# The first chunk's decay attention as blocks of 128 tokens, in a new order of steps

## The chip, the cores and the metric

The kernel runs on one core of a Trainium2 chip. The metric is device time in microseconds (us), the median over several executions. One more execution was taken by the hardware profiler, and every row below is from that one.

## What is computed

The input is q, k, v of 4 batches, 8 heads, 768 tokens and 64 values for each head, a decay `lam` for each head, and two weight matrices in float64. The attention is linear and causal, with a state that decays by `lam` for each token; its output x (3,072 tokens of 512 values) goes through a feed-forward layer of 2,048 hidden values with a softplus.

```python
for b in range(nb):                                   # blocks of 64 tokens
    intra = einsum('bhic,bhjc->bhij', qb, kb) * Dmask  # lam ** (i - j) where i >= j, else 0
    intra = einsum('bhij,bhjd->bhid', intra, vb)
    inter = einsum('bhid,bhde->bhie', qb * lam_pow, kv_state)
    out[:, :, sl] = intra + inter
    kv_state = lam_block * kv_state + einsum('bhsd,bhse->bhde', kb * rev_pow, vb)
x = out.transpose(0, 2, 1, 3).reshape(B * S, H * D)
h = x @ w_in
return softplus(h) @ w_out
```

Nothing in the sum over a block asks for 64 tokens: with a mask over 128 tokens the same result comes from a block of 128.

## The kernel before

The 768 tokens of each batch are cut into 6 chunks of 128, so that a chunk holds 512 tokens over the 4 batches. The attention of one chunk is done in 4 units, one for each pair of heads; unit g belongs to chunk g // 4. A unit's data is 1 MB in two loads of 512 KB (`att`): one with q and k, values along the partitions, one with k and v, tokens along the partitions. Within a unit each chunk is two halves of 64 tokens. `mm_scores` (step `xy`) makes the scores x of both halves and the states' updates y, `mask_scores` (`a`) multiplies the scores by the decay mask, `first_states` or `update_first` and `update_second` (`st`, `dl`, `uh`, `ul`) make the states, and `mm_out` (`z`) adds what comes from the state and from the scores. Before `mm_scores`, `k_decay` (`k`) multiplies k by its decay on ACT, or DVE for unit 0; before `mm_out`, `q_decay` (`q`) multiplies q on DVE. `x_high` (`xh`, ACT) and `x_low` (`xl`, DVE) write the output as two parts, each in the reduced float32 that TensorE reads at full rate (fp32r), so that a product takes three matmuls.

The weights come as float64, 512 KB for each of 16 slices of `w_in` (A0 to A15) and of `w_out` (B0 to B15). `scale` and `round` (ACT), `shift`, `sign` and `add` (DVE) turn the bits into float32, `hi` (ACT) and `lo` (DVE) split it into the two parts. `m f p` and `n f p` (`mlp1`, L412) are three 128x128x512 matmuls of slice f with pair p for chunks 0 and 1; `act`, `ghi`, `glo` are softplus and split of the result; `l2 f` (L425) is the second layer. `sum`, `ph`, `pl`, `snd`, `sA`, `sB` make sums of weight blocks for the later chunks and store them to DRAM, `L2` loads the second layer's weights from there.

All of chunks 0 and 1, and the attention of most later chunks, is issued in an order that is written out by hand as a table of 672 steps (670 after the change); it holds until 234 us. Each engine and each DMA queue takes its instructions in that order, and an instruction that waits holds up all behind it on its engine. Chunks 2 and 3 (pair 1) follow in a loop over 8 steps, in which seven products over block sums (P1 to P7, L593) stand in place of eight, with one unit of attention in each step (`event`). There `box_sums` (L518 and L503 to L506) and `box_parts` (L530) make sums of the second layer's weights on DVE. Chunks 4 and 5 run at last, with `out_product` (L958) for the second layer in the same seven products, in order P1, P6, P2, P7, P5, P4, P3.

SBUF tiles are taken from pools by size (`t8` has 21 buffers of 8 KB for each partition); PSUM has 4 banks `o`, 2 banks `h`, and one tile of 2 banks, `work`, for the outputs z of the units.

Of the kernel before, what the change touches and what calls it, by code (L numbers as in the profile page):

```python
# [15 lines left out]
C = 128  # L16
T = 64
# [13 lines left out]
def decay_attention_softplus_ffn(  # L31
# [103 lines left out]
    for word in "u0 A0 u1".split():  # L135
        load(word)

    spare = t8([128, 4, 512], F32, "spare")
# [15 lines left out]
    ramp = spare[:, 3, 0:T]  # L154
    for s in range(2):
        nc.gpsimd.iota(
            ramp[half(s)], pattern=[[1, T]], base=1 - T, channel_multiplier=1, allow_small_or_imprecise_dtypes=True
        )
    step, *begins = [spare[:, n].rearrange("q (h i) -> q h i", h=H) for n in range(3)]
    nc.gpsimd.memset(begins[1], 0.0)  # L160
    nc.gpsimd.memset(begins[1][:, :, 0:1], 1.0)
    nc.vector.tensor_single_scalar(
        out=begins[0], in_=ramp.rearrange("q (o i) -> q o i", o=1).broadcast_to([128, H, T]), scalar=0.0,
        op=ALU.is_equal,
    )
    nc.vector.tensor_copy(out=step, in_=lam_b.rearrange("q (h o) -> q h o", o=1).broadcast_to([128, H, T]))
    nc.vector.memset(step[:, :, 0:1], 0.0)

    mask = cp.tile([128, H, T], F32, name="mask")

    lp = cp.tile([128, H, T], F32, name="lp")

    def powers(out, n):
        nc.vector.tensor_tensor_scan(
            out=out.rearrange("q h i -> q (h i)"), data0=step.rearrange("q h i -> q (h i)"),
            data1=begins[n].rearrange("q h i -> q (h i)"), initial=0.0, op0=ALU.mult, op1=ALU.add,
        )


    rp1 = cp.tile([128, H], F32, name="rp1")  # L180
    lam_c = cp.tile([128, H], F32, name="lam_c")
    powers(mask, 0)
    nc.vector.tensor_mul(out=rp1, in0=mask[:, :, T - 1], in1=lam_b)
# [76 lines left out]
    def own(g, n, name):  # L260
        if not first_chunk(g):
            return t2([128, B, 2, 64], F32, f"{name}_{g}")
        if g not in spares:
            spares[g] = t8([128, 3, B, 2, 64], F32, f"own_{g}")
        return spares[g][:, n]

    def k_decay(g):
        kd = kds[g] = own(g, 0, "kd")
        if g == 0:
            w = rp1[:, heads(g)].rearrange("q (o t w) -> q o t w", o=1, w=1).broadcast_to([128, B, 2, D])  # L270
            nc.vector.tensor_mul(out=kd, in0=kt_of(g), in1=w)
            return
        for t in range(2):
            h = heads(g).start + t
            nc.scalar.activation(kd[:, :, t], kt_of(g)[:, :, t], AF.Copy, scale=rp1[:, h : h + 1])  # L275

    def q_decay(g):
        qd = qds[g] = own(g, 1, "qd")
        r = hi if first_chunk(g) else slice(0, 128)
        eng = nc.gpsimd if g < 2 else nc.vector  # L280
        w = lp[r, heads(g), :].rearrange("q (o t) i -> q o (t i)", o=1).broadcast_to([r.stop - r.start, B, 2 * T])
        eng.tensor_mul(
            out=qd[r].rearrange("q b t i -> q b (t i)"), in0=q_of(g)[r].rearrange("q b t i -> q b (t i)"), in1=w
        )


# [50 lines left out]
    def carry_states(g, y):  # L337
# [693 lines left out]
```

## Time and profile before

| | |
|---|---|
| median of 3 executions | 579.18 us (578.6 to 579.54) |
| the profiled execution's own time | 580.86 us |
| its span, first to last instruction | 578.8 us |
| TensorE matmuls (PE) | 562.5 us busy, 97% of the span |
| VectorE (DVE), ScalarE (ACT) | 382.8 and 274.2 us busy, 66% and 47% |
| mean granted TensorE clock | 0.993 |
| DMA | 149.70 MB, mean 259 GB/s |

The time of an execution holds 2.1 us beside the span. A busy PE says that a matmul is in flight, and matmuls overlap; what counts is when the next one can start. Idle time matters only on the engine that the others wait for.

### The profile page before, as it was taken

Reading aid. Unit: us, or ns where it says so; the run is one execution under the profiler, and the core shown is the slowest. Engines: PE = TensorE matmul, PEld = TensorE weight load, DVE = VectorE, ACT = ScalarE, POOL = GpSimd, SP = SyncE. Lnnn points to the kernel's source line nnn. Section 1 sums busy time; section 2 is a strip of 40 time slices with the busy share of each in tenths; the row PEclk is TensorE's granted clock in tenths of the full one; section 3 lists DMA queues with packets and bytes.
Section 4 is the critical chain, followed back from the end, with each engine's and each line's share of the span. In section 5 each row is a group of like instructions: output and inputs, shape, how many; then the busy total and the mean of one; then the engine's idle time right before and its main releaser. Section 6 shows DMA issues by size and latency. Waiting matters only on the chain.

```text
span 578.8 us, 12242 instructions
## 1 busy us (share of the span) xinstructions
PE 562.5 (97%) x5208; PEld 459.5 (79%) x5208; DVE 382.8 (66%) x593; ACT 274.2 (47%) x438; POOL 3.9 (1%) x10
## 2 busy tenths in 40 slices
PE   7699999999999999999999999999999999999997
PEld 6567888788887788887878888878888888788885
DVE  5998988687844688466556765549123646748983
ACT  3766668482826454254344443456032334454441
POOL 2000000000000000000000000000000000000000
PEclk9799999999999999999999999999999999999999
DMA  8997399579898899864785787797976246911711
GB/s 289 407 406 303 121 351 340 189 251 330 292 349 326 280 374 398 332 227 193 224 296 172 233 314 228 286 318 290 420 258 221 106 140 212 383 46 59 269 37 73
DMA packets 52678, 149.70 MB, mean 259 GB/s; under 512 B 4496, under 2 KB 20880, under 8 KB 46480
## 3 DMA queue, kind: packets, MB, share of 16 engines
q1 hardware_dynamic: 41040, 135.28, 64.6%
q10 hardware_dynamic: 11584, 13.63, 6.7%
q8 instruction: 41, 0.67, 0.5%
q14 instruction: 13, 0.11, 0.0%
HBM read 111.15 MB, written 37.75 MB: 257 GB/s over the span
## 4 chain that ended last, share of the span: by engine, by line
PE 87%; DMA 8%; DVE 2%; issue 1%; ACT 1%; SPq 1%; ACTq 0%
PE o L425 28%; PE h L412 15%; PE rP L958 13%; PE b L593 11%; PE c L593 7%; PE a L593 7%; DMA att<-in_att 3%; PE x L294 2%; DMA w<-g 2%; PE z L309 2%; DMA raw<-in_wts 2%; PE z L313 1%; PE y L296 1%; DMA out_dram<-ob 1%; DVE box L518 0%
## 5 line engine op out<-in xcount | busy, mean ns | idle before, releaser
L425 PE MATMUL o<-w,g 128*128 128x512 f32 x768 | 185.9, 393 | 0.6 <-DMA w<-g 0.6
L425 PEld LDWEIGHTS o<-w,g 128*128 128x128 f32 x768 | 142.4, 188 | 32.0 <-DMA w<-g 1.1
L412 PE MATMUL h<-x,w 128*128 128x512 f32 x384 | 93.6, 394 | 0.2 <-ACT x L357 0.2
L412 PEld LDWEIGHTS h<-x,w 128*128 128x128 f32 x384 | 70.8, 188 | 16.5 <-ACT x L357 0.6
L958 PE MATMUL rP<-sP,vP 128*128 128x512 f32 x336 | 76.3, 389 | 0.0
L958 PEld LDWEIGHTS rP<-sP,vP 128*128 128x128 f32 x336 | 63.1, 188 | 13.1
L593 PE MATMUL b<-xcP,w1b 128*128 128x512 f32 x192 | 49.1, 391 | 1.2 <-DVE act L895 0.8
L593 PE MATMUL a<-xcP,w1a 128*128 128x512 f32 x192 | 48.8, 389 | 0.0
L326 DVE SCALAR_TENSOR_TENSOR st<-st,lam_c,y 64x256 f32<-64x256 f32 x80 | 35.2, 479 | 14.3 <-PE y L296 13.2
L593 PEld LDWEIGHTS b<-xcP,w1b 128*128 128x128 f32 x192 | 35.8, 188 | 9.8 <-DVE ta L751 1.2
L593 PEld LDWEIGHTS a<-xcP,w1a 128*128 128x128 f32 x192 | 36.0, 188 | 7.6
L321 DVE TENSOR_TENSOR a<-x,mask 128x512 f32<-128x512 f32 x20 | 13.8, 690 | 35.0 <-PE y L296 18.2
L294 PE MATMUL x<-att 64*64 64x64 f32 x768 | 30.7, 226 | 0.0
L294 PEld LDWEIGHTS x<-att 64*64 64x64 f32 x768 | 27.2, 139 | 4.3 <-issue 3.2
L604 DVE TENSOR_TENSOR g<-lb,g 128x512 fp32r<-128x512 f32 x32 | 21.6, 687 | 11.3 <-ACT g L600 11.3
L600 ACT CAST g<-lb 128x512 fp32r<-128x512 f32 x32 | 19.3, 618 | 20.0 <-PE o L425 12.3
L275 ACT ACTIVATE kd<-att,rp 128x256 f32<-128x256 f32 x40 | 18.2, 502 | 20.5 <-DMA att<-in_att 10.3
L895 DVE TENSOR_TENSOR act<-b,ta 128x512 f32<-128x512 f32 x8 | 5.5, 692 | 31.1 <-PE b L593 31.1
L838 ACT CAST sP<-act 128x512 fp32r<-128x512 f32 x32 | 19.2, 619 | 13.0 <-PE rP L958 6.8
L604 DVE TENSOR_TENSOR sP<-act,sP 128x512 fp32r<-128x512 f32 x32 | 20.9, 687 | 6.5 <-ACT sP L838 6.5
L296 PE MATMUL y<-att,kd 64*64 64x64 f32 x576 | 23.1, 220 | 1.5 <-ACT lb L401 1.2
L593 PE MATMUL c<-xcP,w1b 128*128 128x512 f32 x96 | 24.4, 389 | 0.0
(124 smaller groups left out, 791.8 us busy)
## 6 DMA issues: line engine op xcount, KB each, us to landing
att<-in_att SPq DMA_DIRECT2D x48, 512.0 KB, 8.0
w<-g SPq DMA_DIRECT2D x24, 1024.0 KB, 8.3
raw<-in_wts SPq DMA_DIRECT2D x32, 512.0 KB, 10.1
w1a<-g SPq DMA_DIRECT2D x16, 1024.0 KB, 7.1
g<-w SPq DMA_DIRECT2D x24, 512.0 KB, 7.4
w1b<-g SPq DMA_DIRECT2D x16, 768.0 KB, 7.0
g<-box SPq DMA_DIRECT2D x16, 512.0 KB, 9.4
vP<-box ACTq DMA_DIRECT2D x32, 256.0 KB, 6.1
```

Source lines behind the costliest of these rows:

```text
L275: nc.scalar.activation(kd[:, :, t], kt_of(g)[:, :, t], AF.Copy, scale=rp1[:, h : h + 1])
L294: nc.tensor.matmul(x[r, cols], lhsT=k[r, b, t], rhs=q[r, b, t], start=True, stop=True)
L296: nc.tensor.matmul(y[half(1 - s), cols], lhsT=kd[r, b, t], rhs=v[r, b, t], start=True, stop=True,)
L321: nc.vector.tensor_mul(out=a, in0=x.rearrange("q (b t i) -> q b t i", b=B, t=2), in1=m)
L326: nc.vector.scalar_tensor_tensor(out=to[:, :, t], in0=of[:, :, t], scalar=lam_c[r, h : h + 1], in1=u[:, :, t], op0=ALU.mult, op1=ALU.add,)
L412: nc.tensor.matmul(to, lhsT=w[:, i, cs], rhs=x[:, j, :], start=not done and n == 0, stop=len(done) == NP - 1 and n == 2,)
L425: nc.tensor.matmul(outs[c, b], lhsT=g[:, i, b * 128 : (b + 1) * 128], rhs=w[:, j], start=k == 1 and n == 0, stop=k == NF and n == 2,)
L593: nc.tensor.matmul(to, lhsT=w[:, k, n, p * 128 : (p + 1) * 128], rhs=x[:, j, p], start=start and p == 0 and m == 0, stop=p == 1 and m == 2 ...
L600: nc.scalar.copy(out=g[:, 0], in_=l)
L604: nc.vector.tensor_sub(out=g[:, 1], in0=l, in1=g[:, 0])
L838: nc.scalar.copy(out=g[:, 0], in_=of)
L958: nc.tensor.matmul(to, lhsT=w[:, k, x, n * 128 : n * 128 + 128], rhs=g[:, y], start=fresh and i == 0 and m == 0, stop=i == NF // 2 - 1 and ...
```

## The change

Chunk 0's four units take their 128 tokens as one block. The input's layout for them is changed to match on the host, q and k with one head on each half of the partitions, k and v with all 128 tokens along the partitions. `first_scores` makes scores of 128x128 (64 partitions in, 128 columns of weights, 128 columns streamed) into two PSUM banks, one for each head, and y with 128 partitions in and 64 columns; `first_mask` multiplies by a mask of 128 positions, in two instructions; `first_out` has 128 partitions in and 64 columns of weights. No state is needed within the chunk: steps `q 0` to `q 3` and `dl 0` to `dl 3` are gone, and the state that goes to chunk 1 is a copy of y in two instructions. The masks are made over 1,024 columns first (`mask1`, `rpa`), and the ones for 64 tokens after them (`lpset`, `mk64`, `rp1`).

The softplus results of chunk 0's slices 0 to 3 have a buffer of their own (`early`), where one tile held each in turn. The table of steps is a new one. In pair 1 the sums over the second layer's weights of step i are made in step i + 1 in two parts, and `q_decay` follows `event`. Before the last two products P4 and P3 of chunks 4 and 5, one `out_product` of slice 0 is issued ahead of each.

```diff
-        for major in range(2):
+        for major in (1, 0) if g == 0 else (0, 1):
...
-    for word in "u0 A0 u1".split():
+    for word in "".split():
...
+    def first_scores(g, xs, y):
+        q, k = [units[g][:, 0, n].rearrange("q (b i) -> q b i", b=B) for n in range(2)]
+        kd, v = kds.pop(g), part(g, 1, 1)
+        for b in range(B):
+            for t in range(2):
+                r = half(t)
+                nc.tensor.matmul(xs[t][:, b * C : (b + 1) * C], lhsT=k[r, b], rhs=q[r, b], start=True, stop=True)
+        for b in range(B):
+            for t in range(2):
+                nc.tensor.matmul(y[half(t), b * D : (b + 1) * D], lhsT=kd[:, b, t], rhs=v[:, b, t], start=True, stop=True)
+
+    def first_mask(g, xs):
+        a = aa[g] = own(g)[:, 1:3].rearrange("q t (b i) -> q t b i", b=B)
+        for t in range(2):
+            h = heads(g).start + t
+            m = mask1[:, h : h + 1].broadcast_to([128, B, C])
+            nc.vector.tensor_mul(out=a[:, t], in0=xs[t].rearrange("q (b i) -> q b i", b=B), in1=m)
+
+    def first_out(g, w):
+        a, v = aa.pop(g), part(g, 1, 1)
+        for b in range(B):
+            for t in range(2):
+                nc.tensor.matmul(
+                    w[half(t), 0, b * C : (b + 1) * C], lhsT=v[:, b, t], rhs=a[:, t, b], start=True, stop=True
+                )
...
-        st = states[g] = states[g + NP] = th([128, B, 2, D], F32, f"st_{g}")
-        nc.scalar.copy(out=st[hi].rearrange("q b t d -> q (b t d)"), in_=y[hi])
+        st = states[g + NP] = th([128, B, 2, D], F32, f"st_{g}")
+        for t in range(2):
+            nc.scalar.copy(out=st[lo, :, t], in_=y[half(t), 0:256].rearrange("q (b e) -> q b e", b=B))
...
-        l_tiles[f] = tl([128, 512], F32, f"l{f}")
+        if not early:
+            early.append(t8([128, 4, 512], F32, "l0"))
+        l_tiles[f] = early[0][:, f] if f < 4 else tl([128, 512], F32, f"l{f}")
...
-        scale A0, q 0, L A1, L B4, L u3, q 1, k 0, xy 0, L u2, st 0, round A0, L A3, L A2, L A6, L A4, L A5, shift A0,
+        mk64, L A0, lpset, round A0, L u0, L A1, L u1, k 0, scale A0, shift A0, sign A0, scale A1, xy 0, add A0, L u2,
...
-                q_decay(unit)
...
             if i >= 1:
-                box_parts(box_at[i - 1])
+                box_full(box_at[i - 1])
...
             low_of(ga, la)
+            if i >= 1:
+                box_four(box_at[i - 1])
...
                 event(unit)
+                if unit < NG:
+                    q_decay(unit)
                 nxt += 1
             low_of(gb, c21)
...
-            box_sums(box_at[i])
+            if i >= 1:
+                box_parts(box_at[i - 1])
...
-    run(late)
+    banks = {}
+    for n in range(2):
+        banks["a", n] = obank(f"rP1_{n}")
+        out_product("P1", 0, n)
+        run(late, 1)
```

Three places of the new order follow. The first is the queue of loads (SP) at the program's start: att0 is unit 0, raw0 holds A0 and A1, raw1 A2 and A3, raw3 A4 and A5, raw5 A6, raw6 B4. Before:

```order
L84 DMA att0_71<-in_att 128x1024 x2
L124 DMA raw0_74<-in_wts 128x1024
L84 DMA att1_76<-in_att 128x1024 x2
L124 DMA raw0_74<-in_wts 128x1024
L124 DMA raw6_190<-in_wts 128x1024
L84 DMA att3_192<-in_att 128x1024 x2
L84 DMA att2_232<-in_att 128x1024 x2
L124 DMA raw1_238<-in_wts 128x1024 x2
L124 DMA raw5_241<-in_wts 128x1024
L124 DMA raw3_243<-in_wts 128x1024 x2
L84 DMA att4_276<-in_att 128x1024 x2
L84 DMA att5_357<-in_att 128x1024 x2
```

Of the change:

```order
L124 DMA raw0_178<-in_wts 128x1024
L84 DMA att0_185<-in_att 128x1024 x2
L124 DMA raw0_178<-in_wts 128x1024
L84 DMA att1_189<-in_att 128x1024 x2
L84 DMA att2_219<-in_att 128x1024 x2
L124 DMA raw1_222<-in_wts 128x1024 x2
L84 DMA att3_244<-in_att 128x1024 x2
L84 DMA att4_274<-in_att 128x1024 x2
L84 DMA att5_279<-in_att 128x1024 x2
L84 DMA att6_287<-in_att 128x1024 x2
L124 DMA raw3_335<-in_wts 128x1024 x2
L124 DMA raw6_428<-in_wts 128x1024
```

A0 now stands ahead of unit 0, unit 2 ahead of A2 and A3, and units 3 to 6 in a row ahead of A4 and A5. Further on, unit 8 (att8) follows the first slices of B directly, as SP's row 21, where it was row 53, behind stores of weights to DRAM.

The second place is ACT, from the output of unit 1 to that of unit 3: the casts write the output's upper parts x_0 and x_1 (from z1, z2, z3) and the weights' (w), c1 is the `scale` and raw1 the `round` of A2 and A3, c3 and raw3 those of A4 and A5; own and kd are k decays. Before:

```order
L357 CAST x_0_0_313<-z1_331 128x2x4x64
L275 ACTIVATE own_2_403<-att2_232,rp1_151 128x4x64 x2
L334 COPY st_3_407<-y3_365 64x512
L224 CAST w0_319<-c0_185 128x512
L207 ACTIVATE c1_412<-raw1_238 128x1024
L210 ACTIVATE raw1_238<-raw1_238 128x1024
L334 COPY st_2_449<-y2_416 64x512
L207 ACTIVATE c3_452<-raw3_243 128x1024
L357 CAST x_0_1_505<-z2_458 128x2x4x64
L210 ACTIVATE raw3_243<-raw3_243 128x1024
L275 ACTIVATE kd_4_542<-att4_276,rp1_151 128x4x64 x2
L357 CAST x_0_1_505<-z3_516 128x2x4x64
```

Of the change:

```order
L218 ACTIVATE c1_324<-raw1_222 128x1024
L391 CAST x_0_0_247<-z1_315 128x512
L288 ACTIVATE own_3_350<-att3_244,rpa_141 128x4x64 x2
L371 COPY st_2_353<-y2_298 64x4x64 x2
L391 CAST x_0_1_359<-z2_341 128x512
L288 ACTIVATE kd_4_362<-att4_274,rp1_142 128x4x64 x2
L221 ACTIVATE raw1_222<-raw1_222 128x1024
L371 COPY st_3_424<-y3_367 64x4x64 x2
L288 ACTIVATE kd_5_432<-att5_279,rp1_142 128x4x64 x2
L391 CAST x_0_1_359<-z3_444 128x512
L575 CAST box0_0_282<-box0_0_282 128x1024
L235 CAST w1_467<-c1_324 128x1024
```

The `scale` and `round` of A4 and A5 (c3, raw3), which stood ahead of the outputs of z2 and z3, are gone from it and follow later; the k decay of unit 5 (kd_5) and the `ph` cast of box0_0 have come into it.

The third place is DVE in a step of pair 1, from the states of unit 18 to the sum ta, after which the bank b may be added to again (P7). Before, box1_1 being made of the weights of the step itself:

```order
L326 SCALAR_TENSOR_TENSOR st_18_2580<-st_18_2580,lam_c_152,y18_3184 64x4x64 x2
L326 SCALAR_TENSOR_TENSOR st_22_3222<-st_18_2580,lam_c_152,y18_3184 64x4x64 x2
L604 TENSOR_TENSOR g2_3_3126<-tb2_1_3064,g2_3_3126 128x512
L518 TENSOR_TENSOR box1_1_3228<-w2_1_3056 128x1024
L503 TENSOR_TENSOR box1_1_3228<-box1_1_3228 128x256
L504 TENSOR_TENSOR box1_1_3228<-box1_1_3228 128x256
L505 TENSOR_TENSOR box1_1_3228<-box1_1_3228 128x256
L506 TENSOR_TENSOR box1_1_3228<-box1_1_3228 128x256
L282 TENSOR_TENSOR qd_19_3252<-att19_3049,lp_150 128x512
L751 TENSOR_TENSOR ta2_2_3255<-b2_2_3258,ta2_2_3255 128x512
L530 TENSOR_TENSOR box1_1_3228<-box1_1_3228 128x1024
```

Of the change:

```order
L362 SCALAR_TENSOR_TENSOR st_18_2399<-st_18_2399,lam_c_143,y18_3055 64x4x64 x2
L362 SCALAR_TENSOR_TENSOR st_22_3093<-st_18_2399,lam_c_143,y18_3055 64x4x64 x2
L293 TENSOR_TENSOR qd_18_3098<-att18_2728,lp_140 128x512
L653 TENSOR_TENSOR g2_3_2997<-tb2_1_2931,g2_3_2997 128x512
L579 TENSOR_TENSOR box1_0_2948<-box1_0_2948 128x1024
L801 TENSOR_TENSOR ta2_2_3122<-b2_2_3125,ta2_2_3122 128x512
```

Between the states and ta there were a split (g), five sums and a q decay. Now there are a q decay, a split and one subtraction of the previous step's box (L579), which stood behind ta before; the five sums stand behind ta, in two parts.

## Rows read from the trace of the kernel before

**Rows 1.** The page's busy time: us (share of the span) xinstructions.

```profile
PE 562.5 (97%) x5208; PEld 459.5 (79%) x5208; DVE 382.8 (66%) x593; ACT 274.2 (47%) x438; POOL 3.9 (1%) x10
```

**Rows 2.** Busy us of each engine, granted clock, DMA share and GB/s by stretch.

```profile
10.00:40.00 30.00, 21.83 (x604) 17.22 (x604) 27.36 (x45) 21.46 (x35) 1.27 (x1) 0.89 1.03 408
40.00:575.00 535.00, 532.00 (x4441) 435.19 (x4437) 349.64 (x539) 251.42 (x402) 0.00 (x0) 1.00 0.70 252
```

**Rows 3.** PE's waits: for whom, us in total, times, longest.

```profile
PE z L309 <- ACT st L334: 4.3, 2, 2.5
...
PE y L296 <- ACT lb L401: 1.2, 1, 1.2
...
PE b L593 <- DVE act L895: 0.8, 1, 0.8
...
PE o L425 <- DMA w<-g: 0.6, 1, 0.6
PE b L593 <- DVE ta L751: 0.4, 2, 0.2
```

**Rows 4.** The chain that ended last: start, us, what.

```profile
16.72 10.43 DMA raw<-in_wts
...
28.99 1.22 PE h L412 x3
...
101.61 2.72 PE o L425 x12
```

**Rows 5.** ACT's timeline from 10 us: start, us, instruction, wait.

```profile
10.33 0.66 ACT L207 ACTIVATE c<-raw 128x512 f32<-128x512 f32 x1 [8.32 <-DMA raw<-in_wts]
...
27.17 1.16 ACT L207 ACTIVATE c<-raw 128x1024 f32<-128x1024 f32 x1 [1.12 <-DMA raw<-in_wts]
28.35 0.59 ACT L357 CAST x<-z 128x512 fp32r<-128x512 f32 x1
...
29.86 0.91 ACT L275 ACTIVATE kd<-att,rp 128x256 f32<-128x256 f32 x2
...
31.82 1.05 ACT L224 CAST w<-c 128x1024 fp32r<-128x1024 f32 x1
```

**Rows 6.** PE's timeline around 40 us, with the same columns.

```profile
39.98 0.97 PE L412 MATMUL h<-x,w 128*128 128x512 f32 x3
```

**Rows 7.** PE's matmuls up to 40.05 us: xcount | busy, mean ns.

```profile
L412 PE MATMUL h<-x,w 128*128 128x512 f32 x28 | 8.3, 420 | 0.2 <-ACT x L357 0.2
```

**Rows 8.** PE's timeline, one attention step of pair 1.

```profile
246.39 0.34 PE L309 MATMUL z<-qd,st 64*64 64x64 f32 x8
...
247.38 0.22 PE L294 MATMUL x<-att 64*64 64x64 f32 x1
...
248.44 3.06 PE L425 MATMUL o<-w,g 128*128 128x512 f32 x12
```

**Rows 9.** DVE's timeline from 4 us.

```profile
4.06 1.23 DVE L174 TENSOR_TENSOR_SCAN mask<-spare 128x512 f32<-128x512 f32 x1
...
8.07 0.69 DVE L271 TENSOR_TENSOR own<-att,rp 128x512 f32<-128x512 f32 x1 [1.24 <-DMA att<-in_att]
...
34.14 1.22 DVE L228 TENSOR_TENSOR w<-c,w 128x1024 fp32r<-128x1024 f32 x1
```

**Rows 10.** ACT's timeline around 113 us.

```profile
113.10 0.91 ACT L275 ACTIVATE kd<-att,rp 128x256 f32<-128x256 f32 x2 [5.74 <-DMA att<-in_att]
```

**Rows 11.** DVE's timeline at the end of a pair-1 step.

```profile
270.33 1.22 DVE L518 TENSOR_TENSOR box<-w 128x1024 f32<-128x1024 f32 x1
...
273.05 0.68 DVE L282 TENSOR_TENSOR qd<-att,lp 128x512 f32<-128x512 f32 x1
```

**Rows 12.** The page's DMA issues: KB each, median us to landing.

```profile
att<-in_att SPq DMA_DIRECT2D x48, 512.0 KB, 8.0
w<-g SPq DMA_DIRECT2D x24, 1024.0 KB, 8.3
```

**Rows 13.** The page's groups, weight loads of the second layer: xcount | busy, mean ns.

```profile
L425 PEld LDWEIGHTS o<-w,g 128*128 128x128 f32 x768 | 142.4, 188 | 32.0 <-DMA w<-g 1.1
```

More of the change, by code (lines that the diff above doesn't have):

```diff
@@ L152, in decay_attention_softplus_ffn @@
     keep_warm(12)
[L154 to L161, printed above, removed]
+    ramp = masks[:, 3, 0:C]
+    nc.gpsimd.iota(ramp, pattern=[[1, C]], base=1 - C, channel_multiplier=1, allow_small_or_imprecise_dtypes=True)
@@ L174, in powers @@
+    def powers(out, step, begin):
         nc.vector.tensor_tensor_scan(
             out=out.rearrange("q h i -> q (h i)"), data0=step.rearrange("q h i -> q (h i)"),
-            data1=begins[n].rearrange("q h i -> q (h i)"), initial=0.0, op0=ALU.mult, op1=ALU.add,
+            data1=begin.rearrange("q h i -> q (h i)"), initial=0.0, op0=ALU.mult, op1=ALU.add,
         )
[L180 to L183, printed above, removed]
@@ L187, in decay_attention_softplus_ffn, with half_mask, half_ends @@
+    def half_mask():
+        for s in range(2):
+            nc.scalar.copy(out=mask[half(s)], in_=mask1[half(s), :, (1 - s) * T : (2 - s) * T])
+    def half_ends():
+        nc.vector.tensor_mul(out=rp1, in0=mask[:, :, T - 1], in1=lam_b)
     w_pairs, conv = {}, {}
@@ L274, in k_decay @@
             h = heads(g).start + t
-            nc.scalar.activation(kd[:, :, t], kt_of(g)[:, :, t], AF.Copy, scale=rp1[:, h : h + 1])
+            nc.scalar.activation(kd[:, :, t], kt_of(g)[:, :, t], AF.Copy, scale=ends[:, h : h + 1])
     def q_decay(g):
[L278 to L283, printed above, removed]
-        )
+        qd = qds[g] = t2([128, B, 2, T], F32, f"qd_{g}")
+        w = lp[:, heads(g), :].rearrange("q (o t) i -> q o (t i)", o=1).broadcast_to([128, B, 2 * T])
+        nc.vector.tensor_mul(
+            out=qd.rearrange("q b t i -> q b (t i)"), in0=q_of(g).rearrange("q b t i -> q b (t i)"), in1=w
+        )
+    def first_scores(g, xs, y):
[21 more added lines that the diff above has]
+                )
     def mm_scores(g, x, y):
@@ L305, in mm_out @@
             cols = slice(b * 64, b * 64 + 64)
-            for s in range(1 if first_chunk(g) else 0, 2):
+            for s in range(2):
                 r = half(s)
@@ L355, in x_high @@
     def x_high(g, w):
+        if first_chunk(g):
+            nc.scalar.copy(out=x_of(0, g)[:, 0], in_=w[:, 0])
+            return
         nc.scalar.copy(
@@ L458, in begin @@
     def begin(g):
+        if first_chunk(g):
+            xy[g] = [obank(f"x{t}_{g}") for t in range(2)], bank(f"y{g}")
+            first_scores(g, *xy[g])
+            return
         xy[g] = [(obank if g < 2 * NP else bank)(f"{n}{g}") for n in "xy"]
@@ L866, in load_v, with out_product @@
                     )
+    def out_product(p, i, n):
+        g, w, k = splits[p, i], vt[p, i // 4], i % 4
+        fresh = p in ("P1", "P6", "P5")
+        to = banks[{"P1": "a", "P2": "a", "P5": "c", "P3": "c"}.get(p, "b"), n]
+        for m, (x, y) in enumerate(((0, 0), (0, 1), (1, 0))):
+            nc.tensor.matmul(
+                to, lhsT=w[:, k, x, n * 128 : n * 128 + 128], rhs=g[:, y],
+                start=fresh and i == 0 and m == 0, stop=i == NF // 2 - 1 and m == 2, skip_group_check=True,
+            )
     late = []
@@ L951, in take @@
             send(u2, 1, 0, n)
[L953 to L961 removed]
     for j, p in enumerate(order):
[L964 removed]
+        if p == "P6":
             for n in range(2):
[L966 removed]
+                banks["b", n] = obank(f"r{p}_{n}")
         if p == "P5":
@@ L975, in decay_attention_softplus_ffn @@
             split_upto(8 * j + i + 6)
-            for n in range(2):
+            for n in range(2 if j or i else 0):
                 out_product(p, i, n)
```

190 lines of the change are left out of this document (104 added, 86 removed).

## The prediction

> **What bounds the kernel now.** The page's busy times come first [rows 1]: PE is busy for 97% of the span, and the next engine, DVE, for 66%. An average hides the stages, so the windows are next [rows 2]. [...] From 10 to 40 us it is busy for 21.8 of 30 us at a mean clock of 0.89, and the DMA engines are full, at 408 GB/s. So there are two stages: a start in which PE waits, and then a list of matmuls that runs without a break. Whatever is saved in the start moves all the rest forward; in the rest only PE's own waits can be won.
>
> PE's waits [rows 3] name these: 1.2 us behind unit 8's scores (ACT), 0.8 us at the last P4 (DVE), 0.6 us for weights from DRAM, 0.4 us in pair 1 (DVE): 3.0 us. The largest, 4.3 us for the copies of chunk 0's states, lies in the start. The chain [rows 4] shows what paces the start: the load of A5 until 27.15 us, then ACT, then PE. ACT [rows 5] takes A4 and A5 (`scale`) at 27.17 us after a wait of 1.12 us, and only behind it the output of z2, at 28.35 us, for which the matmuls of 28.99 us wait. ACT holds back a result that is ready, because the table has put a late load ahead of it.
>
> How far PE is at 40.0 us: the matmul that starts at 39.98 [rows 6] is the 28th of 128x512 [rows 7]. Done are 27 of them, all of units 0 to 3, the scores of units 4 and 5, and z4. Twelve such matmuls in a row take 2.72 us [rows 4], so 27 take 6.1 us. The scores of a unit take 248.44 - 247.38 = 1.06 us, the outputs 247.38 - 246.39 = 0.99 us [rows 8]. Six scores and five outputs make 11.3 us at most. So 17.4 of 40 us were work, and over 22 us are to be had in principle.
>
> **The start after the change.** The loads keep their pace: 512 KB at 408 GB/s is 1.28 us. The third load had landed at 10.33 us [rows 5], so the n-th lands at 10.33 + 1.28 (n - 3); for the 16th, A5, that gives 26.97 against 27.17 in the trace. In the new order of loads unit 0 is complete with the 3rd (10.3 us), unit 3 with the 12th (21.9), unit 4 with the 14th (24.4), unit 5 with the 16th (27.0), A4 and A5 with the 20th (32.1).
>
> The mask's scan doubles from 1.23 to about 2.5 us, and the ones for 64 tokens come behind it; I put the k decay of unit 0 at 9 us, where it was at 8.07 [rows 9]. That costs nothing, since q and k of unit 0 land at 10.3 us. Units 0 to 2 then follow their loads; the state's copy and the carry between the halves no longer stand between scores and outputs.
>
> What decides is ACT's list around x3, the last piece of chunk 0. With 0.91 us for a k decay, 1.16 for a `scale` or `round`, 0.59 for an output, 1.05 for a cast of 1,024 columns [rows 5], and my estimate of 0.9 us for a state's two copies: k4 at its load, 24.4 to 25.3; `round` of A2 and A3 to 26.5; state 3 to 27.4; k5 to 28.3; the output of z3 to 28.9; `ph` to 29.9; `hi` of A2 and A3 to 31.0. DVE needs four pieces of about 0.7 us behind z3 and a `lo` of 1.22 [rows 9], which ends at 32.2. PE fills this time: z3 ends near 28.0, nine matmuls of slice 1 end at 30.1, `m 0 3` at 30.8, the scores of unit 5 at 31.9, z4 at 32.9. Slice 3 can begin (its `lo` is ready), and six of its matmuls end at 34.3. This is the point that the kernel before reaches at 40.0: 5.7 us earlier. Next, A4 and A5 land at 32.1; scale, three DVE steps, `hi` and `lo`, behind the other work of both engines, end at 41.2, and PE asks for them at 41.3. There is no margin, so I take off 0.7 us: **5.0 us** gained.
>
> Bounds: 5.7 us if nothing is late. [...]
>
> **The 128-token blocks on PE.** A float32 product of 64x64 runs four at a time today: 32 products in 1.06 us [rows 8], so a round of four takes 0.13 us. A unit of chunk 0 has 32 products for scores and 24 for outputs: 1.06 + 0.75 to 1.0 us. Now it has 8 with 128 columns streamed, two at a time if the halves of the array work side by side, 4 x 0.26 = 1.06 us; 8 with 64 columns, 0.53 us; 8 with 128 columns again, 1.06 us. That is 2.65 us for 1.9, or 0.75 us more, four times. The first three units lie where PE waits for loads (8 us idle from 10 to 40 us [rows 2]); the fourth is in the walk above. The trace shows no tile of 64x128 or 128x64. One at a time, each unit would take 5.3 us (see the rivals). I take them as side by side, since the nearest rows show tiles that share neither rows nor columns doing so.
>
> [...]
>
> **The other terms.** Unit 8's k decay waited 5.74 us for its load [rows 10], which stood behind stores; it is now the 31st and 32nd load, at about 47 us. That takes away the wait of 1.2 us. In pair 1 the five sums (1.22 us and four shorter ones, 270.33 to 273.05) and the q decay (0.68) stand ahead of ta [rows 11], and PE loses 0.4 us in two steps [rows 3]; a subtraction of about 1.2 us comes ahead of it in their place, so some 1.5 us are won on DVE and the 0.4 us go. The sums now lie while P5 to P7 run; if DVE were late there, P4's sum would be late next. Before the last P4 three matmuls of P1, 0.68 us, fill the wait of 0.8 us [rows 3]; I count 0.7. The early buffer costs PE nothing: it lets the banks go without waiting for the splits.
>
> A new wait: the load of the second layer's slices 2 and 3 (`L2 1`) now stands right ahead of `p2 3`. Its buffer comes free with `p2 7`; from there to `p2 3` PE has 24 matmuls (5.4 us) and two scores and two outputs (4.1 us), 9.5 us. The load takes 8.3 us in the middle [rows 12], behind up to 2 MB of others (5 us). PE waits for 0 to 4 us, where it waits for 0.6 us now; I count 1.2 us more.
>
> **Sum.** 580.86 - 5.0 (start) - 1.2 (unit 8) - 0.4 (pair 1) - 0.7 (last P4) + 1.2 (`L2 1`) = 574.8 us for a profiled execution like this one, 6.1 less. Its time is 1.7 us above the median of the runs shown, 579.18; for the median I say **573.1 us**. By the bounds above the likeliest case runs from 570 to 575.2 us.
>
> **Rivals.** *The lead is given back.* PE is 5.7 us ahead at 34 us, but the weights only 3.2 (`lo` of A2 and A3 ended at 35.36 [rows 9], now 32.2). If conversion on ACT and DVE, or stores and loads up to 234 us, cannot follow, the lead falls to what they allow, 3.2 us, with the waits above partly back: 575.2 to 577.9. Against it: DMA is at 0.70 on average from 40 us on [rows 2], and the first six slices of both chunks hold 144 matmuls, 33 us of work. Chance 0.2.
>
> *The tiles run one at a time: slower.* [...] The gain of the start is gone from 5.7 us on the path, some 1.4 us a unit. For it: no row shows tiles of these shapes. Against it: the rows of 64x64 tiles, four at a time. Chance 0.07. [...]
>
> *The start does not change.* Loads fill the DMA engines in both orders, and if the first matmul of the unbroken list waits for A4 and A5 wherever they stand, nothing moves: 578.6 to 580. Against it: before, A5 had long landed at 40 us. Chance 0.05.
>
> Some other wait in the 670 new places, above 5 us: 0.05.
>
> **Numbers.** The forecast has 0.63. Faster by over 0.2% (1.2 us, about what a measurement of this kernel can tell): 0.63 + 0.2 = 0.83; within 0.2%: 0.06; slower: 0.11. For 8 in 10 the range takes the forecast's case, up to its far end with the whole `L2 1` wait gone (569.8), and most of the given-back case: 569.8 to 577.6 us.
>
> **What would show it.** PE's 28th matmul of 128x512 at 34 to 35 us; four matmuls of `first_scores` starting in pairs, with a unit's scores in about 1.1 us; `lo` of A2 and A3 near 32; no wait of PE in 110 to 120 us and none for DVE in pair 1; a wait of up to 4 us for `w<-g` shortly before pair 1. I am wrong if pairs of the new tiles don't overlap, if the clock is low past 22 us, or if PE has new waits for weights between 40 and 100 us.

## The result, and the profile after

The changed kernel takes 570.88 us, median of 4 executions (569.9 to 573.75), against 579.03 us for the kernel before: ratio 0.9867, 95% interval 0.9831 to 0.9903. The forecast was 573.1 us, 569.8 to 577.6. The profiled execution took 569.9 us, the one of before 580.86, so these two differ by 11.0 us where the medians differ by 8.15: one lies 1.0 us below its median, the other 1.8 above. What follows of traces accounts for the 11.0.

The page's busy times, for [rows 1]:

```profile
PE 556.8 (98%) x4952; PEld 458.4 (81%) x4952; DVE 379.2 (67%) x590; ACT 272.4 (48%) x444; POOL 1.1 (0%) x7
```

The windows, with the columns of [rows 2]:

```profile
10.00:40.00 30.00, 27.73 (x556) 22.47 (x555) 27.18 (x43) 24.14 (x43) 0.00 (x0) 1.00 1.03 418
40.00:564.00 524.00, 521.89 (x4293) 430.05 (x4291) 344.42 (x536) 244.54 (x397) 0.00 (x0) 1.00 0.70 256
```

PE's waits, for [rows 3]:

```profile
PE x L303 <- DMA att<-in_att: 1.5, 1, 1.5
PE z L319 <- DVE x L412: 1.5, 2, 0.8
...
PE o L467 <- DMA w<-g: 1.4, 1, 1.4
PE z L319 <- DVE own L313: 0.8, 2, 0.6
PE a L642 <- ACT ta L799: 0.6, 1, 0.6
```

From 10 to 40 us PE is busy for 27.73 us where it was for 21.83, and the granted clock is 1.00 where it was 0.89. The waits for states, for unit 8 and at the last P4 are gone; `w<-g`, the load `L2 1` of the second layer's weights, has grown from 0.6 to 1.4 us, and a wait for `ta` is new.

How large the start's gain is can be read without an estimate, from the point at which as much is left. Windows of PE from such a point on, first before, then after (columns as in [rows 2]; the last two windows reach past the end):

```profile
40.31:580.00 539.69, 531.82 (x4437) 434.91 (x4435) 350.02 (x540) 251.23 (x402) 0.00 (x0) 1.00 0.70 250
```

```profile
34.16:580.00 545.84, 527.88 (x4437) 434.93 (x4435) 350.16 (x542) 249.29 (x404) 0.00 (x0) 1.00 0.69 251
```

In both, 4,437 recorded matmuls are touched by the window; counted by their starts, 2,132 of 128x512 and 2,304 of 64x64 are left behind 40.32 us before and behind 34.17 us after. The start has gained 6.15 us. Call this moment the **equal point**, and what follows, up to the last matmul, the **rest**: 534.4 us before and 529.6 after. The lead at more such pairs of equal remainders, counted in the two traces:

| left: 128x512, 64x64 | before us | after us | lead us |
|---|---|---|---|
| 2,132, 2,304 (equal point) | 40.32 | 34.17 | 6.15 |
| 2,063, 1,984 | 62.86 | 55.64 | 7.22 |
| 1,848, 1,984 | 111.65 | 104.75 | 6.90 |
| 1,836, 1,920 (behind unit 8's scores) | 117.12 | 108.70 | 8.42 |
| 1,632, 1,600 | 170.14 | 160.56 | 9.58 |
| 1,535, 1,280 | 199.64 | 188.26 | 11.38 |
| 1,487, 1,024 (behind `w<-g`) | 215.54 | 205.49 | 10.05 |
| 1,397, 896 (behind `ta`) | 238.37 | 229.03 | 9.34 |
| 1,193, 512 | 292.48 | 282.14 | 10.34 |
| 347, 0 (behind the last P4's wait) | 496.28 | 484.92 | 11.36 |
| the last matmul | 574.75 | 563.76 | 10.99 |

So 6.15 us come from the start and some 4.9 from the rest, where the forecast had 5.0 and 1.1.

In the start, PE's and ACT's timelines (as [rows 5, 8]):

```profile
13.76 1.16 PE L303 MATMUL x<-att 64*128 64x128 f32 x16
14.85 0.69 PE L306 MATMUL y<-att,own 128*64 128x64 f32 x16
15.46 1.16 PE L303 MATMUL x<-att 64*128 64x128 f32 x16
...
18.10 1.09 PE L319 MATMUL z<-own,att 128*64 128x128 f32 x16 [0.76 <-DVE x L412]
19.13 0.97 PE L454 MATMUL h<-x,w 128*128 128x512 f32 x3
```

```profile
27.59 0.59 ACT L391 CAST x<-z 128x512 fp32r<-128x512 f32 x1 [0.77 <-PE z L319]
28.07 1.05 ACT L575 CAST box<-box 128x1024 fp32r<-128x1024 f32 x1
29.02 1.05 ACT L235 CAST w<-c 128x1024 fp32r<-128x1024 f32 x1
```

The 16 matmuls of a line are 8 products, two recorded matmuls for each. A unit's scores take 14.85 - 13.76 = 1.09 us, its y 15.46 - 14.85 = 0.61, its outputs 19.13 - 18.10 = 1.03: 2.73 us, 2.65 forecast. ACT takes the output of z3 at 27.59 us, and ends it, `ph` and `hi` of A2 and A3 0.7 to 0.9 us ahead of the prediction's walk.

### The profile page after: what moved, and what is told of

Read it like the earlier page. It is cut to its first block, busy times and chain, and to the rows that moved or that the text cites. A ratio compares the mean times of both kernels' runs of the same rounds, so it can differ in the third digit from the quotient of the medians.

```text
span 567.8 us, 11744 instructions
## 1 busy us (share of the span) xinstructions
PE 556.8 (98%) x4952; PEld 458.4 (81%) x4952; DVE 379.2 (67%) x590; ACT 272.4 (48%) x444; POOL 1.1 (0%) x7
## 4 chain that ended last, share of the span: by engine, by line
PE 90%; DMA 7%; ACT 1%; SPq 1%; DVE 0%; issue 0%; ACTq 0%
PE o L467 28%; PE h L454 16%; PE rP L931 13%; PE b L642 11%; PE a L642 7%; PE c L642 7%; DMA att<-in_att 3%; PE x L330 2%; DMA raw<-in_wts 2%; DMA w<-g 2%; PE z L345 2%; PE z L349 1%; PE y L332 1%; PE z L319 0%; ACT c L218 0%
## 5 line engine op out<-in xcount | busy, mean ns | idle before, releaser
L454 PE MATMUL h<-x,w 128*128 128x512 f32 x384 | 91.5, 392 | 0.0
L362 DVE SCALAR_TENSOR_TENSOR st<-st,lam_c,y 64x256 f32<-64x256 f32 x72 | 31.7, 480 | 9.3 <-PE y L332 8.3
L642 PE MATMUL b<-xcP,w1a 128*128 128x512 f32 x96 | 24.4, 389 | 0.0
L642 PE MATMUL c<-xcP,w1a 128*128 128x512 f32 x96 | 24.4, 389 | 0.0
L579 DVE TENSOR_TENSOR box<-box 128x1024 fp32r<-128x1024 f32 x16 | 19.5, 1221 | 7.1 <-ACT box L575 6.9
```

The costliest lines, as they stand in the source:

```text
L362: nc.vector.scalar_tensor_tensor(out=to[:, :, t], in0=of[:, :, t], scalar=lam_c[r, h : h + 1], in1=u[:, :, t], op0=ALU.mult, op1=ALU.add,)
L454: nc.tensor.matmul(to, lhsT=w[:, i, cs], rhs=x[:, j, :], start=not done and n == 0, stop=len(done) == NP - 1 and n == 2,)
L579: nc.vector.tensor_sub(out=lo.bitcast(F32R), in0=lo, in1=hi)
L642: nc.tensor.matmul(to, lhsT=w[:, k, n, p * 128 : (p + 1) * 128], rhs=x[:, j, p], start=start and p == 0 and m == 0, stop=p == 1 and m == 2 ...
```

## The experiments

All ratios are to the kernel before on the same chip. The runs are from several chips, on which the median of before goes from 579.0 to 579.8 us, so rows compare by their ratios. The last two columns are of the profiled execution.

| run | median us | ratio (95%) | equal point | rest |
|---|---|---|---|---|
| before | 579.0 to 579.8 | 1 | 40.3 | 534.4 |
| the change | 570.88 | 0.9867 (0.9831 to 0.9903) | 34.2 | 529.6 |
| e1_order | 584.14 | 1.0075 (1.0058 to 1.0092) | 44.5 | 531.1 |
| e2_blocks | 578.25 | 0.9980 (0.9971 to 0.9989) | 39.3 | 532.8 |
| e3_start | 572.91 | 0.9875 (0.9858 to 0.9892) | 34.2 | 532.6 |
| e4_nohoist | 571.33 | 0.9864 (0.9844 to 0.9884) | 33.9 | 534.1 |
| e5_serial | 572.30 | 0.9873 (0.9860 to 0.9886) | 36.6 | 529.8 |
| e6_fix | 567.84 | 0.9798 (0.9782 to 0.9815) | 34.2 | 529.0 |
| e7_act_early | 577.39 | 0.9962 (0.9949 to 0.9975) | 40.0 | 531.0 |
| e8_act_late | 579.82 | 1.0002 (0.9993 to 1.0011) | 39.8 | 533.4 |
| e9_order2 | 584.06 | 1.0079 (1.0063 to 1.0095) | 44.4 | 533.4 |
| e10_three | 567.72 | 0.9802 (0.9788 to 0.9815) | 34.2 | 527.7 |
| e11_start | 567.13 | 0.9797 (0.9784 to 0.9811) | 33.9 | 526.8 |
| e12_split | 571.68 | 0.9887 (0.9848 to 0.9925) | 35.9 | 529.4 |

**The order or the blocks?** Two kernels, each with one half of the change.

*e1_order*: before, with the new table (`q g` and `dl g` put back, `st 0` and `st 2` ahead of their `z`), the new order of loads, and the early buffer:

```diff
-    for word in "u0 A0 u1".split():
+    for word in "".split():
...
-        scale A0, q 0, L A1, L B4, L u3, q 1, k 0, xy 0, L u2, st 0, round A0, L A3, L A2, L A6, L A4, L A5, shift A0,
+        L A0, round A0, L u0, L A1, L u1, q 0, k 0, scale A0, shift A0, sign A0, scale A1, xy 0, st 0, add A0, L u2,
```

> The new order of steps and loads and the early buffer, with chunk 0 still in halves of 64 tokens and pair 1 and the last P4 as before. Theory A (the order makes the start's gain: each load's conversion stands behind the results that are ready when it lands): PE reaches the remaining work of 2,132 matmuls of 128x512 some 4 us earlier than before; with unit 8's load early (1.3 us won) and the late load of the second layer's slices 2 and 3 (0.8 us lost) the median is 574 to 575 us. Theory B (the 128-token blocks make it, by taking the states out of the chain between scores and outputs): the start stays within 1 us of before, and the median is 577.5 to 579.5 us.

*e2_blocks*: the changed kernel with the table of before, less the steps that the blocks do without, and with the loads, the buffers, pair 1 and the last P4 of before:

```diff
-        mk64, L A0, lpset, round A0, L u0, L A1, L u1, k 0, scale A0, shift A0, sign A0, scale A1, xy 0, add A0, L u2,
+        mk64, lpset, scale A0, L A1, L B4, L u3, k 0, xy 0, L u2, st 0, round A0, L A3, L A2, L A6, L A4, L A5, shift A0,
```

> The 128-token blocks alone, in the order of before, with the steps that are no longer needed left out of it. Theory A (order): ACT still waits for A5 at 27 us ahead of the output of z2, and PE has about 0.75 us more to do for each unit; the wait of 4.3 us for states is gone but a later one takes its place: 577 to 580 us. Theory B (blocks): the wait of 4.3 us goes for good, and the median is about 574 us.

The blocks alone gain 1.5 us, the order alone loses 4.35, both together gain 6.9 (e3_start, below); these three are from one chip. Neither theory holds: A had the order at 574 to 575 us, B had the blocks at 574. The order of steps, the order of loads and the early buffer go together in these runs, so which of them carries the order's part is not shown. In e2_blocks the waits for states fall from 4.3 to 1.6 us, and waits for masked scores and outputs stand in their place, as A said of this half:

```profile
PE z L319 <- DVE own L313: 2.4, 3, 2.1
PE h L452 <- ACT st L371: 1.6, 1, 1.6
...
PE h L452 <- ACT x L391: 1.0, 1, 1.0
```

In e1_order PE stops, and then runs at a granted clock of 0.50; its timeline:

```profile
33.44 0.37 PE L309 MATMUL z<-own,st 64*64 64x64 f32 x2 [3.09 <-issue]
```

The windows around it:

```profile
30.00:34.00 4.00, 0.91 (x35) 0.82 (x28) 1.84 (x3) 0.00 (x0) 0.00 (x0) 0.88 1.03 406
34.00:39.00 5.00, 5.00 (x25) 3.92 (x19) 3.12 (x4) 2.48 (x3) 0.00 (x0) 0.50 1.02 409
```

The stop of 3.1 us is in the middle of one unit's outputs, and "issue" says that no operand was missing. Behind it PE works at a granted clock of 0.50 until 39.9 us. A matmul of 128x512 is in flight for 0.79 us there (34.48), where it was for 0.40 ahead of the stop (29.29), so that about half of these 6.4 us is lost. Stop and clock are 6.3 us of the 10.4 by which its equal point lies behind the change's (44.53 us for 34.17); 3.2 us were lost ahead of the stop (the seventh matmul of 128x512 starts at 28.72 us, in the change at 25.54).

*e9_order2* looks at that stop. Its table steps, one on a line:

```diff
-  xy 4
   m 0 2
+  m 1 2
+  m 1 0
+  m 1 1
   z 3
+  xy 4
```

> The kernel of e1_order (new order, halves of 64 tokens) with nine matmuls of 128x512 moved ahead of unit 3's outputs and unit 4's scores behind them, so that fewer of the short 64x64 instructions follow each other. In e1_order PE stopped for 3.1 us in the middle of unit 3's outputs, at 30.1 us, with all operands ready, while a packet of 16 KB on the instruction queue landed at 32.2; then the granted clock was 0.5 from 34 to 39 us. Theory D (PE ran out of fetched instructions, and the clock fell behind that): the stop shrinks below 1.5 us, the clock stays at 1.0 from 30 to 40 us, and the median falls from 584.1 by 4 to 6 us, to 578 to 580 us. Theory B (the chain through the states is what makes the order slow): the median stays at 583 to 585 us.

The stop has moved, and has not shrunk:

```profile
40.61 0.27 PE L313 MATMUL z<-a,att 64*64 64x64 f32 x2 [3.22 <-issue]
```

The median is where B had it, and D's remedy failed. But what D says of the stop holds again: in e1_order 1,217 instructions of PE (matmuls, weight loads and a few others) were recorded before it, here 1,473, 256 more; each time a 16 KB packet of the instruction queue is on its way (31.07 to 32.17 us, and 38.12 to 39.23) and PE goes on 1.3 to 1.4 us behind its end. The packet that ends ahead of the stop's end in e1_order starts only at 31.07 us, 4.0 us after PE has begun the 256 instructions that end at the stop, at 27.06. Moving steps only moved the end of these 256 to another step.

The other traces settle what the stops are. In all 14 there are 15 with "issue" that are longer than 0.25 us, two of them in the kernel before:

```profile
32.25 0.27 PE L296 MATMUL y<-att,kd 64*64 64x64 f32 x1 [0.37 <-issue]
...
39.23 0.21 PE L309 MATMUL z<-qd,st 64*64 64x64 f32 x1 [0.92 <-issue]
```

Each of the 15 stands where the count of PE's recorded instructions is 193 or 194 above a multiple of 256, and ends 1.25 to 1.62 us behind the end of a 16 KB packet; in no trace do 256 instructions counted from there start earlier than 1.23 us behind their packet. I read these stops as waits of PE for its instructions. Ahead of the stop of e1_order it went through 256 in 3.3 us (27.06 to 30.35), while the next packet ended 5.1 us after 27.06. In the change the 256 from 25.34 us take 6.4 us, and the packet ends after 4.3: a unit of chunk 0 has 48 matmuls there in place of 112.

*e12_split* adds PE instructions to the changed kernel, with its work and steps as they are:

```diff
-                nc.tensor.matmul(xs[t][:, b * C : (b + 1) * C], lhsT=k[r, b], rhs=q[r, b], start=True, stop=True)
+                for n in range(2):
+                    to = xs[t][:, b * C + n * T : b * C + n * T + T]
+                    nc.tensor.matmul(to, lhsT=k[r, b], rhs=q[r, b, n * T : n * T + T], start=True, stop=True)
```

and the same in `first_out`.

> The changed kernel with each product of chunk 0's scores and outputs issued as two of 64 columns: the same work and the same chain of steps in the same order, but 16 products more for each unit, 256 PE instructions more with their weight loads (two for a product, and as many loads). Theory D (in the start PE is short of fetched instructions when many short ones follow each other, since the packets of 16 KB wait among the loads, and this is why the order needs the blocks): PE stops once or twice for 1 to 3 us at such a packet between 15 and 40 us, and the median rises by 3 us or more, to 574 us or more. Theory B (only the chain of steps matters): the units' products take at most some 0.3 us more each, partly where PE waits for loads, and the median stays within 1 us, below 572 us.

571.68 us, and no stop in the trace: by the terms stated, D fails. It is not refuted, though. The 256 instructions that start at 33.45 us start 1.23 us behind the end of their packet, as early as any in the 14 traces; and of the six executions one took 573.12 and one 578.88 us, at lower granted clocks (0.997 and 0.994), of which there is no trace. And the added instructions came slowly, as the timeline shows:

```profile
13.69 2.05 PE L305 MATMUL x<-att 64*128 64x64 f32 x32
15.67 0.69 PE L308 MATMUL y<-att,own 128*64 128x64 f32 x16
...
18.78 1.15 PE L323 MATMUL z<-own,att 128*64 128x64 f32 x32
19.86 0.96 PE L456 MATMUL h<-x,w 128*128 128x512 f32 x3
```

The 32 score instructions take 1.98 us, where 32 of z go in 1.08, and in the units of 64-token halves 128 recorded matmuls start in 2 us. That PE stops between one 256 and the next where the packet comes late is shown by the 15 stops. How much of the order's need for the blocks is this, and how much the steps for states that they do away with, is not.

**Are the tiles side by side?** *e5_serial*, in scores, y and outputs alike:

```diff
-        for b in range(B):
-            for t in range(2):
+        for t in range(2):
+            for b in range(B):
```

> The changed kernel with the two heads of chunk 0's products one after the other, so that neighbours in PE's list always use the same part of the array, in scores, y and outputs. Theory A (neighbours overlap because they are in different parts, by rows for the scores and by columns for y and outputs): a unit takes about 4.3 us in place of 2.75, three of the four units lie partly where PE waits for loads, and the median rises by some 3 us to 574 us. Theory C (only tiles that share no rows overlap, so y and outputs were never side by side): only the scores grow, by 0.6 us a unit, and the median rises by 0.6 to 1 us, to 571.7 us.

```profile
12.10 1.69 PE L319 MATMUL z<-own,att 128*64 128x128 f32 x16 [1.03 <-DVE own L313]
13.71 1.71 PE L303 MATMUL x<-att 64*128 64x128 f32 x16
15.35 0.97 PE L306 MATMUL y<-att,own 128*64 128x64 f32 x16
16.25 1.71 PE L303 MATMUL x<-att 64*128 64x128 f32 x16
```

All three grow: scores from 1.09 to 1.64 us, y from 0.61 to 0.90, outputs from 1.03 to 1.61; a unit takes 4.15. One after the other, a float32 product streams 128 columns in 0.205 us (1.64 / 8), where an fp32r matmul streams 512 in 0.227 [rows 4]; this is what the runs show of fp32r's full rate. Tiles that share all their rows and differ in columns, those of y and outputs, do run side by side, so theory C falls: by it y and outputs would have stayed as they were. The equal point is 2.4 us later. The median is 1.4 us higher, 0.65 of it the chip's (before takes 579.68 us there, 579.03 on the change's chip), and the intervals of the ratios overlap; A had said 3.

**ACT's list.** *e7_act_early* undoes one choice of the new order, *e8_act_late* makes it in the old one; table steps, one on a line, first e7_act_early:

```diff
+  scale A4 A5
   xh 3
+  round A4 A5
   xl 3
...
-  scale A4 A5
...
-  round A4 A5
```

> The changed kernel with the scale of A4 and A5 ahead of the output of unit 3 on ACT, where the kernel before had it ahead of such outputs, and the round right behind that output. Theory A (ACT's list decides): unit 3's output, at 27.6 us in the changed kernel, waits until A5 has landed (30.9) and been scaled, 32 us; PE has matmuls until about 30 and then waits some 3 us for it: 573 to 574.5 us. Rival: PE finds other work, or A4 and A5 being ready earlier makes up for it: 570.5 to 571.5 us.

ACT's timeline in e7_act_early:

```profile
30.83 1.12 ACT L218 ACTIVATE c<-raw 128x1024 f32<-128x1024 f32 x1 [4.04 <-DMA raw<-in_wts]
31.97 0.58 ACT L391 CAST x<-z 128x512 fp32r<-128x512 f32 x1
```

Its windows, with PE's clock:

```profile
30.00:32.00 2.00, 0.00 (x0) 0.00 (x0) 0.00 (x0) 1.15 (x2) 0.00 (x0) 1.00 1.02 418
32.00:34.00 2.00, 1.39 (x3) 0.79 (x3) 1.41 (x3) 2.00 (x3) 0.00 (x0) 0.52 1.02 418
34.00:38.00 4.00, 4.00 (x130) 3.69 (x130) 2.92 (x5) 2.77 (x5) 0.00 (x0) 0.50 1.02 418
```

Theory A has the direction and the place to a tenth (31.97 for 32), but the price is 5.9 us at the equal point where it said 3 (6.5 between the medians, 0.65 of it the chip's): PE waits 2.8 us and then works at a granted clock of 0.50 until about 38.9 us (from the 0.77 granted for 38 to 40), which, at half the pace, is another 3. With two steps moved, nearly all of the start's gain is gone: the equal point is at 40.0 us.

*e8_act_late*, in the kernel before:

```diff
-  scale A4 A5
...
   xh 2
...
-  round A4 A5
...
   xh 3
+  scale A4 A5
   xl 3
   hi A2 A3
+  round A4 A5
```

> The kernel before with one edit: the scale and round of A4 and A5 stand behind the outputs of units 2 and 3 on ACT. Theory A (ACT's wait for A5 at 27 us held back outputs that were ready): unit 2's output comes 2 us earlier, and 1 to 2 us of the start are won: 577 to 578 us. Rival: A4 and A5 are late next, by as much: 578.7 to 579.5 us.

```profile
27.45 0.59 ACT L357 CAST x<-z 128x512 fp32r<-128x512 f32 x1 [1.30 <-PE z L313]
```

No change. With the load out of the way the output of z2 waits for PE, and comes at 27.45 us instead of 28.35 [rows 5]: 0.9 us earlier, where 2 were expected. At the equal point 0.55 us of it are left, and in the median of 12 executions nothing. What held the start in the kernel before was not this wait alone.

**The small terms.** *e3_start* takes pair 1's edits and the early `out_product` out of the changed kernel, *e4_nohoist* only the latter:

```diff
-        out_product("P1", 0, n)
-        run(late, 1)
+    run(late)
```

> The changed kernel with pair 1's sums and q decay and the last P4 as they were. By the stalls that went from the trace (0.75 us in pair 1, 0.68 at the last P4) the median is 1.4 us above the changed kernel's 570.9: 572.3 us. Rival: these stalls are made up for elsewhere, since the end hangs on something else: 570.9 us.

> The changed kernel without the three matmuls of P1 ahead of each of the last two products. The wait before the last P4 is back at 0.7 to 0.8 us, and nothing else moves: 571.6 us. Rival: the matmuls were never in the way of the end: 570.9 us.

The wait at the last P4 is back in both traces, at 0.8 us, and the two of 0.2 us for `ta` in e3_start. The medians can't tell: by ratio they lie 0.0008 above the change and 0.0003 below it (0.5 and -0.2 us), well inside its interval, so signs and sizes rest on the traces alone. The trace of e4_nohoist, of an execution 2.8 us above its median, shows something else. DVE's timeline, and PE's:

```profile
337.99 1.23 DVE L564 TENSOR_TENSOR box<-w 128x1024 f32<-128x1024 f32 x1 [5.58 <-DMA vP<-box]
339.13 0.68 DVE L811 TENSOR_TENSOR tb<-b,ta 128x512 f32<-128x512 f32 x1
```

```profile
339.87 1.66 PE L642 MATMUL b<-xcP,w1b 128*128 128x512 f32 x6 [2.99 <-DVE tb L811]
```

The first of pair 1's sums, which the change moved ahead of `tb`, waits for a store that still reads its buffer, and PE waits with it.

**A better version.** *e6_fix* takes on the two new waits:

```diff
-            if unit is not None and unit < NG:
-                k_decay(unit)
...
             nc.vector.tensor_add(out=u2, in0=b_, in1=p1)
+            if unit is not None and unit < NG:
+                k_decay(unit)
```

and in the table `p2 10`, second-layer matmuls of slice 10, stands ahead of `p2 3`.

> The changed kernel with two moves: pair 1's k decay behind the first sum with ta instead of ahead of the copy of P1, and twelve matmuls that have their weights (p2 10) ahead of those that wait for the load of slices 2 and 3. Theory A (both are waits of one queue behind a late load, with nothing else late): the waits of 1.4 and 0.6 us go and the median is 568.9 us. Rival: the loads themselves are the bound there, and the next matmuls wait in their place: 570.5 to 571 us.

3.0 us faster than the change, and the intervals of the two ratios don't meet. ACT's timeline, of the change and of e6_fix:

```profile
227.27 0.91 ACT L288 ACTIVATE kd<-att,rp 128x256 f32<-128x256 f32 x2 [13.16 <-DMA att<-in_att]
228.08 0.56 ACT L799 COPY ta<-a 128x512 f32<-128x512 f32 x1
```

```profile
225.65 0.59 ACT L797 COPY ta<-a 128x512 f32<-128x512 f32 x1 [9.01 <-PE a L642]
228.69 0.91 ACT L288 ACTIVATE kd<-att,rp 128x256 f32<-128x256 f32 x2 [2.45 <-DMA att<-in_att]
```

The decay of a unit whose load was late stood ahead of the copy that PE needed. Both waits are gone from its trace, which makes 2.0 of the 3.0 us; the rest is within what medians of 4 executions scatter. (The execution profiled is 1.3 us above its median, with 0.7 us for `g` and a stop of 1.0 us for instructions at 169 us in its waits, so its own rest is only 0.6 us shorter.)

*e10_three* moves the sum of e4_nohoist's trace, on top of e6_fix:

```diff
-            if i >= 1:
-                box_full(box_at[i - 1])
...
             low_of(ga, la)
             if i >= 1:
+                box_full(box_at[i - 1])
                 box_four(box_at[i - 1])
```

> The kernel of e6_fix with the first of pair 1's five sums moved from ahead of the sums that PE waits for to behind them. In one profiled execution of e4_nohoist that sum waited 5.6 us for a store of its buffer, at 336 us, and PE lost 3.0 us there. Theory A (this wait makes the scatter of 3 to 4 us between executions of the changed kernel): the median stays at 567 to 567.8 us and no execution lies more than 1.5 us above the median. Rival: the sums are then late for the next product, and the median rises by 0.5 us or more.

567.72 us; its 4 executions lie within 1.25 us (567.1 to 568.35), those of the change within 3.85. Those of e6_fix, without this move, lie within 2.5. That fits, with few executions.

*e11_start*, on top of it (table steps):

```diff
-  sum 0
...
   z 1
+  xh 1
   scale A2 A3
...
-  xh 1
   xl 1
+  sum 0
```

> The kernel of e10_three with two moves in the start: the sums of weight blocks (sum 0) on DVE from ahead of unit 0's low part to behind unit 1's, and unit 1's output on ACT ahead of the scale of A2 and A3, which waits for a load. PE's two waits there, 0.8 and 0.7 us for the low parts, go. Theory A (PE's waits in the start add up, since all behind moves forward): 1.0 to 1.4 us less than e10_three. Rival: the loads of unit 3 and of A2 and A3 set the pace, and the same time is waited behind them: within 0.4 us of e10_three.

567.13 us, 0.6 less, between the two and inside both intervals; the equal point is 0.35 us earlier, as the rival has it. Of PE's two waits of 0.8 and 0.7 us, read in the change and in e6_fix, one of 0.5 is left; but e10_three's own trace has only that one too, so that the moves did it is not shown, and a wait of 0.3 us for a k decay is new. This is the fastest kernel here, 2.0% under the kernel before (0.9784 to 0.9811).

## Why the prediction was right, and where it was off

**The start, 5.0 us: right, low by 1.15.** The walk gave 5.7 and I took off 0.7 because A4 and A5 would be asked for with no margin. No such wait came: PE has none from 22 to 200 us but where it changes between kinds of matmuls, and its 28th of 128x512 starts at 33.9 us. The loads ran at 418 GB/s, not 408, so that A5 lands at 30.8 us in place of 32.1 (e7_act_early's wait ends there). A clock that is low past 22 us, which would have made me wrong, did not come: the granted clock is 1.00 from 10 to 40 us. The far end of the likeliest case, 575.2 us, is an estimate of mine that no run shows; the runs of the change itself go up to 573.75. What a low clock can cost is seen in e7_act_early, e1_order and e9_order2, where one wait of about 3 us costs another 1.7 to 3.2 us by a granted clock of 0.50.

**Why there is a gain.** "ACT holds back a result that is ready" was right as a danger of the new order (e7_act_early: 5.9 us) and wrong as the cause in the old one (e8_act_late: none). And the prediction told the start as one effect of the order, with the blocks as a price of 0.75 us a unit. The runs show an interaction: neither half gains more than 1.5 us alone. With blocks the order keeps PE without a wait behind 22 us, and the granted clock at 1.00; without them it loses 3.2 us in the first units and stops for instructions, and the clock adds to the longest stop. PE's supply of instructions has no place in the prediction: it counts the blocks' time on PE, not that they are less than half as many matmuls.

**The blocks' price, 2.65 us a unit: right**, 2.73. The rival "one at a time: slower" has its own measure now: 4.15 us a unit, not 5.3, and a kernel at most 1.4 us above the change, not slower than before. It was over-priced: in that trace the granted clock is 1.00 all through the start, and over half of the extra 5.7 us lies where PE waited anyway (the equal point moves by 2.4).

**Unit 8, pair 1, the last P4** (1.2, 0.4, 0.7 us): the waits are gone as said; the lead rises by 1.5, 1.0 and, up to the last P4, 1.0 at these places.

**`L2 1`, +1.2 us: right.** 1.4 us where 0.6 stood before is 0.8 more in this pair of traces; the eight traces that have this load ahead of `p2 3` show 1.4 to 2.2 us, the three with the old order 0 to 0.6.

**Not foreseen.** A wait of 0.6 us for `ta`, by the same mechanism that the prediction told for unit 8, a k decay ahead of its load on ACT, at the one place where pair 1's loads come late (0 to 1.4 us in other traces of this order). The rival of "some other wait" was priced at over 5 us; this one is small. Larger is a gain that I did not count: behind the equal point PE changes between attention and 128x512 products 20 times, where it did 28 times, because outputs and the next scores now often stand together. A change into a group and out of it adds 0.22 us to the starts (0.318 and 0.148 us in place of two ordinary steps), and the second matmul of 128x512 behind a group starts 0.338 us after the first where 0.227 is usual: 0.33 us a group. The chain of the change shows the part that lies behind a group, on the first of two times twelve matmuls, which follows one:

```profile
127.23 2.95 PE o L467 x12
...
133.57 2.72 PE o L467 x12
```

0.33 us for 8 groups is 2.7 us. Of the 4.85 us of the rest, waits are 1.2 (counted in starts), groups 2.7, and 0.9 I can't assign. This part comes with the order: e1_order, with the old blocks and the same 20 groups, has a rest 3.3 us shorter than before.

**The lead given back** (0.2) did not happen: from the equal point on the lead grows, but for the two new waits and some tenths.

**Sum.** For the profiled executions -11.0 us where -6.1 was forecast; for the medians -8.15. The difference of 2.85 us between the two is scatter of single executions. The range held by its terms for the start and the waits; the groups' 2.7 us, which the sum has at nothing, took the median to near its lower end. The change's own scatter, 569.9 to 573.75, has no source in its own trace; traces of its variants show two, the sum that waits for a store (3.0 us in e4_nohoist) and stops for instructions near 169 us (0.4 to 1.0 us in e3_start, e4_nohoist and e6_fix).

## What to carry to other kernels

When two halves of a change are judged by one walk through a start that is bound by loads, test each half alone: a step that makes results ready early and an order that asks for them early may gain only together. In an in-order queue, look at every instruction that waits for a load or a store and ask what stands right behind it; here three such places cost 0.6, 3.0 and 5.9 us, and each hung on where one or two lines stand. Price a wait of about 3 us of TensorE in the start at more than its length: three such waits here cost another 1.7 to 3.2 us. Where a trace has TensorE stop with its operands ready, count its instructions up to the stop and look at the packets of the instruction queue (here 193 or 194 above a multiple of 256, and packets of 16 KB).

## What the hardware showed that I had not expected

- Three waits of 2.8 to 3.2 us in the start were followed by 3.4 to 6.8 us at a granted clock of 0.50, though PE was busy for nearly all of that time (e1_order until 39.9 us, e7_act_early 32.1 to 38.9, e9_order2 41.5 to 44.9). The wait of 2.5 us that ends at 26.1 us in the kernel before was not.
- PE stopped for up to 3.2 us with its operands ready, always 193 or 194 instructions above a multiple of 256, until 1.25 to 1.62 us behind the end of a 16 KB packet of instructions (15 stops in 8 of the 14 traces).
- The scores' tiles of 64x128 take the same time for 64 streamed columns as for 128: 32 instructions in 1.98 us (0.062 each) against 16 in 1.09 (0.068), while those of 128x64 take half (0.034 against 0.064).
- Tiles that share all rows and differ in columns overlap: y 0.61 us in turn, 0.90 one head after the other.
